# Three planner prices, the choice of the planner's pass, and elementwise work moved from GpSimd to VectorE

## The chip, the cores and the metric

The program runs on one core of one Trainium2 chip. The metric is the device time of one execution in microseconds; the kernel before was timed three times and its median is used.

## The reference, cut to what matters

A linear attention with a decaying state over 768 steps (4 batches, 8 heads, head size 40) feeds two feed-forward layers of 320 by 2048, with different gates.

```python
for t in range(S):                                    # S = 768, state is D x D per head
    y[:, :, t] = einsum('bhd,bhde->bhe', rt, state)
    Sa = einsum('bhde,bhe->bhd', state, at)
    state = state * wt[:, :, None, :] - einsum('bhd,bhe->bhde', Sa, bt) + einsum('bhd,bhe->bhde', vt, kt)
x = y.transpose(0, 2, 1, 3).reshape(3072, 320)
h = x @ moe_w_in;  x = (h * cos(h)) @ moe_w_out
h = x @ moe2_w_in; x = (h * clip(h + 3, 0, 6) / 6) @ moe2_w_out
```

The feed-forward weights arrive as 64-bit floats.

## The kernel before

The sequence is cut into 12 chunks of 64 steps; a chunk and a batch together are a unit `n` (48 of them). For each unit the attention loads operands (`pA`), scales and splits them into two fp16 parts (`pB`), transposes them by DMA (`pT`), forms a 64 by 64 system (`pC`), and later solves and applies it (`cV`, `cU`, `cA`, `cG`, `cF`); the state between chunks is carried in `S8` (`cS`, `cF`), and its fp16 copies go out by `cST`. Per chunk, `iA` to `iC` invert triangular blocks on VectorE, column by column, and `iD`/`iE` join the blocks with 64 small fp32 products of 32 by 32 (32 calls each, four partition groups, tile `q`), which give the tile `TT`.

The feed-forward layers run per chunk: `mA` forms `h` in PSUM (16 matmuls of 128 by 128 by 256), applies the gate on ScalarE and VectorE and splits the result into `ghl`; `mB` multiplies it with `wout` into `acc`. Layer 0 and layer 1 alternate on TensorE with the attention of later chunks.

The weights come in 44 pieces (22 per layer). `ld_w` loads a piece as pairs of 32-bit words, `prep_w` builds fp32 values from them: ScalarE takes the absolute value of the high word, VectorE shifts (`tensor_scalar`) and puts the sign in, and then the top three bits of the low word have to come in. Since `E_LO` is 1 for both layers, `cnt` always reaches 1 and this last step goes by ScalarE (a scaled copy of the low word to an integer) and an integer add on GpSimd. After that a cast and a subtraction make the two fp16 parts.

No engine's order is written by hand. All calls go to a recorder, `Plan`: `rec` gives each a price in ns, `order` works out an order, and `emit` issues it. Lines that matter:

```python
ALTS = {"ANY": ("DVE", "POOL"), "CPY": ("DVE", "ACT")}
```

A call on `nc.either` that isn't a copy has the engine ANY, and one that is a copy has CPY: the planner chooses the engine as it goes. `order` alternates 50 times (`PASSES`) between `forward`, a list schedule in modelled time by priority, and `backward`, which gives the next priorities; the start times of the last `forward` are the order, and the engine of each ANY and CPY call is the one of that pass. In `forward`, `pick` gives GpSimd an ANY call when VectorE isn't running an operation marked `port` (no operand in PSUM), and only if `o["alt"] - spare <= POOL_GAIN * o["c"]`; while GpSimd runs, VectorE gets calls without that mark alone. The order has no effect on the chip but through the sequence on each engine and on the SP queue, which issues nearly all DMAs; semaphores do the rest.

The price of a DMA on SP's queue is 475 or 650 by the partitions of its tile, and 1175 or 1244 for a transposing one. A fp32 matmul costs `max(2 * (5 + 0.835 * m), 4 * n / 2.4)`, which is 63.4 for the 32 by 32 product; the shape change adds 192 to a block of them. Every operation is issued through line 459 (or 455, where a copy falls to ScalarE), so the profile's groups are told apart by tile names. Tile `wstat` is a second staging place beside `wout`; `Tt` also holds the fp16 state parts, `S8a` also the small tiles `xs` and `ul`.

Of the kernel before, what the change touches and what calls it, by code (L numbers as in the profile page):

```python
# [12 lines left out]
U32 = mybir.dt.uint32  # L13
AF = mybir.ActivationFunctionType
ALU = mybir.AluOpType
# [23 lines left out]
W_HUGE = 122880.0  # L39
W_SCALE = 2.0 ** -111  # L40
W_TOP = 2.0 ** -96
E_LO = 1.0, 1.0
T_R, T_0, T_D1, T_D2, T_W0, T_W0E, T_W1, T_W1E = 78, 70, -8, -6, -59, -30, -5, 11
T_P, D_P, T_I, D_I, T_C, D_C, T_M2, T_WM, LAG = 48.0, 2.0, 36.0, 7.0, 26.05, 2.1, 8, 150, 2
E_WC, E_WL, E_DM, E_NT, E_GL, E_KB, E_AR, E_XS, E_MA = 1, 0, 0, 0, 0.5, 0, 0, 0, 0
# [32 lines left out]
        return t  # L78


ALTS = {"ANY": ("DVE", "POOL"), "CPY": ("DVE", "ACT")}
T_SHAPE = 96.0
FULL = (128, 128)
POOL_GAIN = -0.03
OFFSET = 110
LAT = {"PE": 190, "DVE": 125, "ACT": 140, "POOL": 70}

# [1 line left out]
class Plan:  # L89
# [68 lines left out]
    def rec(self, attr, eng, name, a, kw):  # L158
        i = len(self.ops)
        outs, ins = [], []  # L160
        if a and isinstance(a[0], bass.AP):
            outs.append(a[0])
            ins += [x for x in a[1:] if isinstance(x, bass.AP)]
        for k, x in kw.items():
            if isinstance(x, bass.AP):
                (outs if k in ("out", "accum_out") else ins).append(x)
        n = max(_free(x) for x in outs[:1] + (ins if name in ("tensor_reduce", "activation") else []))
        dma = None
        if name.startswith("dma"):
            sb = outs[0] if outs[0].tensor.__class__.__name__ == "Tile" and outs[0].tensor._space != DRAM else ins[0]  # L170
            c = 475.0 if sb.shape[0] in (32, 128) or ins[0].ap[0][0] == 0 else 650.0
            by = 1
            for k in outs[0].shape:
                by *= k
            by *= mybir.dt.size(outs[0].dtype)
            if name == "dma_start":
                run = _run(outs[0], ins[0])
                run = min(run, 20480)
                dma = by / run * (9 + run * 0.045) / 16
            else:  # L180
                r, w = ins[0].shape[0], by // 2 // ins[0].shape[0]
                dma = w / 128 * 204 * (1 if r >= 64 else r / 128)
                c = 1244.0 if r == 128 and w >= 1024 else 1175.0
        elif eng == "PE":
            m = _free(ins[0])
            c = max(n / 2.4 + 2.5, 25.0 if m == 128 else 32.0)
            if ins[0].dtype == F32:
                c = max(2 * (5 + 0.835 * m), 4 * n / 2.4)
            shape = tuple(32 if x <= 32 else 64 if x <= 64 else 128 for x in (ins[0].shape[0], _free(ins[0])))
        elif eng in ("DVE", "ANY"):  # L190
            c = 70 + n * 1.042
            es = max(mybir.dt.size(x.dtype) for x in outs + ins)
            if name == "tensor_copy":
                c = 70 + n * (0.26 if es == 2 else 0.52)
            elif name == "tensor_tensor" and n > 512 and any(len(x.ap) > 2 and abs(x.ap[-1][0]) > 4 for x in ins):
                c = 70 + n * 1.906
            elif name == "tensor_scalar":
                c = 70 + n * 0.52
            elif name == "reciprocal":
                c = 70 + n * 6.3  # L200
            elif name == "tensor_tensor_scan":
                c = 70 + n * 2.08
            if any(_free(x) == 1 for x in ins):
                c += 60
        elif eng == "ACT":
            c = 95 + n * 0.833
            if "accum_out" in kw:
                c += 93
            elif "bias" in kw:
                c += 50  # L210
            elif ins[0].tensor._space == PSUM:
                c -= 42

        turn = name == "tensor_copy" and n > 512 and abs(outs[0].ap[-1][0]) > 4
        if turn:
            c = 70 + n * 1.906
        rate = 2.56 if any(abs(x.ap[-1][0]) > 4 for x in ins) else 2.1 if all(mybir.dt.size(x.dtype) == 4 for x in outs + ins) else 1.88
        cp = 36 + n * 0.83 if name == "memset" else 150 + n * (rate if name == "tensor_tensor" else 3.4)
        if eng == "POOL":
            c = cp  # L220
        elif eng == "ANY" and name == "tensor_copy":
            eng, cp = "CPY", 70 + n * 1.906 if turn else 95 + n * 0.833
        merge = eng == "PE" and self.ops and self.ops[-1]["eng"] == "PE" and self.ops[-1]["grp"] == (self.group, outs[0].tensor.name)
        if merge:
            i -= 1
            o = self.ops[i]
            o["c"] += c + (T_SHAPE if shape != o["shape"] else 0)
            o["shape"] = shape
        else:
            o = dict(eng=eng, c=c, alt=cp if eng in ALTS else None, dma=dma, deps=set(), prio=self.prio, calls=[],  # L230
                     grp=(self.group, outs[0].tensor.name), i=i, port=False, shape=FULL, off=0)
            self.ops.append(o)
            if eng == "PE" and shape != FULL:
                o["c"] += 2 * T_SHAPE
                o["shape"] = shape

            o["off"] = OFFSET if any(_part(x) for x in outs[:1] + ins) else 0
            o["port"] = name not in ("memset", "tensor_reduce", "reciprocal") and all(getattr(x.tensor, "_space", None) != PSUM for x in ins)
        o["calls"].append((attr, name, a, kw))
        for x in ins:  # L240
            self.touch(x, False, i, o["deps"])
        for x in outs:
            self.touch(x, True, i, o["deps"])

    def order(self):

        ops = self.ops
        n = len(ops)
        for o in ops:
            for k in ("c", "alt", "dma"):  # L250
                o[k] = None if o[k] is None else int(o[k] + 0.5)

        known = [0] * n
        pred = []
        users = [[] for _ in ops]
        for o in ops:
            i, a, keep = o["i"], 0, []
            for d in sorted(o["deps"], reverse=True):
                if not a >> d & 1:
                    keep.append(d)  # L260
                    users[d].append(i)
                    a |= known[d] | 1 << d
            known[i] = a
            pred.append(keep)

        tail = [0] * n
        nxt = 0
        for o in reversed(ops):
            i = o["i"]
            m = max([tail[u] for u in users[i]], default=0)  # L270
            moe = o["eng"] == "PE" and o["grp"][0][0] in ("mA", "mB")
            if moe:
                m = max(m, nxt - LAT["PE"])
            tail[i] = m + (o["c"] + LAT.get(o["eng"], 0) if o["dma"] is None else 2200 + o["dma"])
            if moe:
                tail[i] -= o["c"] * SHARE // 100
                nxt = tail[i]
        pr = [-t for t in tail]
        for k in range(PASSES):
            start = self.forward(pr, pred, users)  # L280
            if k < PASSES - 1:
                pr = self.backward(start, pred, users)
        return sorted(range(n), key=lambda i: (start[i], i))

    def backward(self, start, pred, users):
# [61 lines left out]
    def forward(self, pr, pred, users):  # L347

        ops = self.ops
        n = len(ops)  # L350
# [14 lines left out]
        def pick(e, t):  # L365
# [10 lines left out]
            if e == 3:  # L376
                if port[1] > t:
                    return None
                spare = max(0, free[1] - t) + sum(ops[i]["c"] for _, i in q[1] if i not in gone and not ops[i]["port"])
                for _, i in sorted(q[3]):  # L380
                    if i in gone:
                        continue
                    o = ops[i]
                    if o["eng"] == "POOL" or o["alt"] - spare <= POOL_GAIN * o["c"]:
                        return i
                return None
            return q[e][0][1]

        def arrive(u):
# [113 lines left out]
def kernel(  # L503
# [87 lines left out]
    def dp(name, frac):  # L591
        return nc.either

    cnt = {}
    ldq = nc.sync
    tq = nc.sync

# [166 lines left out]
    def prep_w(m, kind, i):  # L764
# [4 lines left out]
        else:  # L769
# [5 lines left out]
            nc.vector.tensor_scalar(out=x, in0=x, scalar1=3, scalar2=None, op0=ALU.logical_shift_left)  # L775
            nc.vector.scalar_tensor_tensor(out=x, in0=hi, scalar=-(1 << 31), in1=x,
                                           op0=ALU.bitwise_and, op1=ALU.bitwise_or)
            cnt[m] = cnt.get(m, 0.0) + E_LO[m]
            if cnt[m] < 0.999:
                nc.vector.scalar_tensor_tensor(out=x.bitcast(U32), in0=lo.bitcast(U32), scalar=29, in1=x.bitcast(U32),  # L780
                                               op0=ALU.logical_shift_right, op1=ALU.bitwise_or)
            else:
                cnt[m] -= 1.0
                nc.scalar.activation(out=lo, in_=lo.bitcast(U32), func=AF.Copy, scale=2.0 ** -29)
                nc.gpsimd.tensor_tensor(out=x, in0=x, in1=lo, op=ALU.add)
        if kind == "i":
            q, k = divmod(i, 3)
            sl = slice(q * 512, q * 512 + 512)
# [725 lines left out]
```

## Time and profile before

| | us |
|---|---|
| median of three runs | 1210.59 (1209.37 to 1214.22) |
| the profiled execution | 1216.33 |
| its span, first to last instruction | 1214.4 |

Busy time of the engines in that span: PE (TensorE) 873.8 us, DVE (VectorE) 1020.0, ACT (ScalarE) 808.1, POOL (GpSimd) 187.0; the mean granted clock of TensorE is 0.945 of 2.4 GHz. A busy time counts an instruction from its start to its end, also where it stood still in between. SPq in a row is SP's queue: the time that SP took to issue a DMA, which the table of busy times leaves out.

### The profile page before, as it was taken

To read this page: it belongs to the slowest core of one execution; us is meant where nothing else is said; L and a number is where in the kernel's file an instruction comes from. 1 tells how busy PE (TensorE), PEld (TensorE's weight loads), DVE (VectorE), ACT (ScalarE), POOL (GpSimd) and SP (SyncE) were. 2 spreads that over 40 slices of the span, in tenths; PEclk is the share of its full clock that TensorE was granted. 3 is DMA by queue.
4 is the path that set the end of the run, shared out by engine and by line. 5 is a ranking of instruction groups with operands and counts; after the bars stand their busy time and mean duration, and the time that the engine had idled before them with its cause. 6 is when DMAs were issued, how large, how long until landed. Compare 5 with 4: busy or idle time off the path is not lost.

```text
span 1214.4 us, 29691 instructions
## 1 busy us (share of the span) xinstructions
PE 873.8 (72%) x11378; PEld 697.5 (57%) x11378; DVE 1020.0 (84%) x2328; ACT 808.1 (67%) x1695; POOL 187.0 (15%) x221
## 2 busy tenths in 40 slices
PE   0000113357967899799897898999979979999994
PEld 0000112355755677587675677776758758778873
DVE  7699999899999899599895899989969969885652
ACT  5563689888887679487595776867857737464341
POOL 3320111232222101020030020200200114200000
PEclk9999999977987999899999899999989989999998
DMA  6998778997878749777578687776775743512010
GB/s 213 243 195 172 167 218 179 207 202 171 176 152 151 146 85 142 159 130 135 121 128 148 121 144 152 132 148 109 140 162 101 110 99 69 104 37 49 1 25 15
DMA packets 477818, 162.65 MB, mean 134 GB/s; under 512 B 447941, under 2 KB 460273, under 8 KB 477282
## 3 DMA queue, kind: packets, MB, share of 16 engines
q1 hardware_dynamic: 477378, 160.00, 65.9%
q8 instruction: 91, 1.49, 0.5%
q14 instruction: 61, 0.50, 0.2%
q10 hardware_dynamic: 288, 0.67, 0.1%
HBM read 80.09 MB, written 25.61 MB: 87 GB/s over the span
## 4 chain that ended last, share of the span: by engine, by line
DVE 28%; PE 20%; DMA 9%; SPq 6%; issue 5%; ACT 4%; POOL 1%; DVEq 0%; ACTq 0%; POOLq 0%
PE h L459 10%; PE acc L459 7%; SPq L459 6%; DVE Tt L459 4%; DVE s L459 4%; DVE tmp L459 3%; DVE ghl L459 3%; DVE S8a L459 3%; PE t L459 2%; DMA x1T<-S8a 2%; DVE GF L459 1%; DVE FS L459 1%; DVE gm L459 1%; DMA Lt<-Ls 1%; DVE xy L459 1%
## 5 line engine op out<-in xcount | busy, mean ns | idle before, releaser
L459 PE MATMUL acc<-wout,ghl 128*128 128x320 f16 x2304 | 363.3, 306 | 15.5 <-DVE ghl L459 8.3
L459 PEld LDWEIGHTS <-win 128*128 128x128 f16 x3328 | 317.7, 103 | 86.9 <-issue 39.4
L459 PEld LDWEIGHTS <-ghl 128*128 128x128 f16 x2304 | 218.6, 100 | 98.5 <-DVE ghl L459 11.2
L459 PE MATMUL h<-x1T,win 128*128 128x256 f16 (+1 forms) x1664 | 206.1, 287 | 32.6 <-DVE s L459 25.1
L459 ACT ACTIVATE s<-h,cvec 128x512 f32<-128x512 f32 x192 | 130.5, 682 | 136.6 <-PE h L459 66.7
L459 PE MATMUL h<-x2T,win 128*128 128x256 f16 (+1 forms) x1664 | 184.7, 266 | 3.7 <-DVE s L459 3.7
L459 DVE TENSOR_TENSOR ghl<-s,ghl 128x512 f16<-128x512 f32 x177 | 122.0, 690 | 3.2 <-ACT ghl L455 1.4
L459 DVE TENSOR_TENSOR tmp<-Tt,Lt 128x126 f32<-128x126 f32 (+22 forms) x372 | 100.5, 270 | 13.0 <-DMA Lt<-Ls 8.1
L459 DVE TENSOR_TENSOR Tt<-Tt,tmp 128x126 f32<-128x126 f32 (+22 forms) x372 | 103.4, 278 | 4.4
L459 DVE SCALAR_TENSOR_TENSOR s<-h,s 128x512 f32<-128x512 f32 x96 | 65.5, 686 | 42.3 <-ACT s L459 40.5
L459 PE MATMUL p<-ART,KBT 120*128 120x64 f16 x384 | 22.3, 208 | 104.5 <-DMA ART<-ARs 73.3
L455 ACT ACTIVATE ghl<-s 128x512 f16<-128x512 f32 x126 | 78.3, 624 | 27.6 <-DVE s L459 21.4
L459 DVE SCALAR_TENSOR_TENSOR s<-s,h 128x512 f32<-128x512 f32 x96 | 64.8, 678 | 25.0 <-ACT s L459 25.0
L459 PEld LDWEIGHTS <-KBT 120*128 120x128 f16 x384 | 19.6, 107 | 108.6 <-DMA KBT<-KBs 88.7
L459 PE MATMUL t<-E,GF 128*128 128x40 f16 x1152 | 45.7, 183 | 37.7 <-DVE GF L459 37.3
L459 PE MATMUL t<-FS,NT 128*128 128x40 f16 x768 | 37.5, 183 | 37.8 <-DVE FS L459 19.5
L459 PEld LDWEIGHTS <-GF 128*128 128x128 f16 x1152 | 38.0, 98 | 45.7 <-DVE GF L459 25.5
L459 PEld LDWEIGHTS <-TT 64*128 64x128 f16 (+1 forms) x768 | 28.2, 97 | 61.1 <-issue 28.7
L459 POOL TENSOR_TENSOR wout<-wout 128x512 int32<-128x512 int32 (+1 forms) x28 | 45.6, 1637 | 97.7 <-ACT wout L459 72.1
L459 PEld LDWEIGHTS <-NT 128*128 128x128 f16 x768 | 32.6, 98 | 35.4 <-issue 27.2
L459 PEld LDWEIGHTS <-ART 120*64 120x64 f16 (+1 forms) x704 | 43.6, 106 | 7.9 <-issue 4.1
L459 PE MATMUL q<-Lt 32*32 32x32 f32 x1536 | 23.9, 204 | 31.3 <-DMA Lt<-Tm 13.9
(159 smaller groups left out, 1675.1 us busy)
## 6 DMA issues: line engine op xcount, KB each, us to landing
raw<-in_arbk_dram SPq DMA_DIRECT2D x46, 320.0 KB
v<-in_vv_dram SPq DMA_DIRECT2D x96, 80.0 KB
pip<-Dec SPq DMA_DIRECT2D x46, 160.0 KB
wout<-in_moe_w_in_dram SPq DMA_DIRECT2D x12, 512.0 KB
Ls<-LN SPq DMA_DIRECT2D x48, 128.0 KB
Lt<-Ls SPq DMA_DIRECT2D x48, 128.0 KB
TT<-Thl SPq DMA_DIRECT2D x12, 512.0 KB
wstat<-in_moe_w_out_dram SPq DMA_DIRECT2D x10, 512.0 KB
```

The source lines that it names most:

```text
L455: self.nc.scalar.activation(func=AF.Copy, **kw)
L459: getattr(getattr(self.nc, attr), name)(*a, **kw)
```

## The change

Six edits. (1) ANY may go to VectorE alone, and the rule with `POOL_GAIN` goes. (2) In `prep_w` the low word's bits come in with one VectorE `scalar_tensor_tensor` (shift right by 29, or) in place of the ScalarE copy and the GpSimd add; `E_LO` and `cnt` go. (3) A plain DMA costs 520, 640, 740 or 960 ns of SP's queue by the number of contiguous runs and the partitions. (4) A transposing DMA costs 1310 or 1390. (5) A fp32 matmul with 32 columns of weights costs 30. (6) `order` keeps the start times and the engines of the pass with the smallest modelled last start.

```diff
-ALTS = {"ANY": ("DVE", "POOL"), "CPY": ("DVE", "ACT")}
+ALTS = {"ANY": ("DVE",), "CPY": ("DVE", "ACT")}
-POOL_GAIN = -0.03
...
-            c = 475.0 if sb.shape[0] in (32, 128) or ins[0].ap[0][0] == 0 else 650.0
...
+                k = by // run
+                c = 520.0 if k <= 64 else 640.0 if k <= 128 else 960.0 if sb.shape[0] == 40 else 740.0
                 run = min(run, 20480)
...
-                c = 1244.0 if r == 128 and w >= 1024 else 1175.0
+                c = 1390.0 if r == 128 and w >= 1024 else 1310.0
...
-                c = max(2 * (5 + 0.835 * m), 4 * n / 2.4)
+                c = 30.0 if m == 32 else max(2 * (5 + 0.835 * m), 4 * n / 2.4)
...
+        best = None
         for k in range(PASSES):
             start = self.forward(pr, pred, users)
+            if best is None or max(start) < best[0]:
+                best = max(start), start, [o["on"] for o in ops]
             if k < PASSES - 1:
                 pr = self.backward(start, pred, users)
+        _, start, on = best
+        for o, e in zip(ops, on):
+            o["on"] = e
...
-                spare = max(0, free[1] - t) + sum(ops[i]["c"] for _, i in q[1] if i not in gone and not ops[i]["port"])
-                for _, i in sorted(q[3]):
-                    if i in gone:
-                        continue
-                    o = ops[i]
-                    if o["eng"] == "POOL" or o["alt"] - spare <= POOL_GAIN * o["c"]:
-                        return i
-                return None
             return q[e][0][1]
...
-            cnt[m] = cnt.get(m, 0.0) + E_LO[m]
-            if cnt[m] < 0.999:
-                nc.vector.scalar_tensor_tensor(out=x.bitcast(U32), in0=lo.bitcast(U32), scalar=29, in1=x.bitcast(U32),
-                                               op0=ALU.logical_shift_right, op1=ALU.bitwise_or)
-            else:
-                cnt[m] -= 1.0
-                nc.scalar.activation(out=lo, in_=lo.bitcast(U32), func=AF.Copy, scale=2.0 ** -29)
-                nc.gpsimd.tensor_tensor(out=x, in0=x, in1=lo, op=ALU.add)
+            nc.vector.scalar_tensor_tensor(out=x.bitcast(U32), in0=lo.bitcast(U32), scalar=29, in1=x.bitcast(U32),
+                                           op0=ALU.logical_shift_right, op1=ALU.bitwise_or)
```

## Rows read from the trace of the kernel before

**Rows 1.** The page: busy shares in 40 slices of the span, in tenths.

```profile
PE   0000113357967899799897898999979979999994
...
DVE  7699999899999899599895899989969969885652
...
POOL 3320111232222101020030020200200114200000
PEclk9999999977987999899999899999989989999998
```

**Rows 2.** Busy time of each engine in three stretches of the span.

```profile
0.00:400.00 400.00, 148.76 (x2344) 122.74 (x2345) 360.81 (x744) 288.30 (x585) 95.99 (x102) 0.92 0.83 187
400.00:1100.00 700.00, 627.02 (x8161) 497.35 (x8159) 603.59 (x1472) 483.77 (x1037) 90.96 (x119) 0.96 0.67 122
1100.00:1214.40 114.40, 97.99 (x880) 77.43 (x878) 55.57 (x113) 36.08 (x74) 0.00 (x0) 0.95 0.10 20
```

**Rows 3.** The page: the chain that ended last, share of the span.

```profile
DVE 28%; PE 20%; DMA 9%; SPq 6%; issue 5%; ACT 4%; POOL 1%; DVEq 0%; ACTq 0%; POOLq 0%
```

**Rows 4.** Groups of POOL by form: count, busy us, mean ns, idle before.

```profile
L459 POOL TENSOR_TENSOR wout<-wout 128x512 int32<-128x512 int32 x22 | 35.3, 1606 | 88.7 <-ACT wout L459 70.2 <-DVE NT L459 7.1 <-issue 5.1
L459 POOL TENSOR_TENSOR wstat<-wstat 128x512 int32<-128x512 int32 x14 | 21.4, 1529 | 107.4 <-ACT wstat L459 34.4 <-DVE tmp L459 29.7 <-DVE S8a L459 20.0
L459 POOL TENSOR_TENSOR S8a<-S8a,pd 40x320 f32<-40x320 f32 x19 | 20.0, 1059 | 47.1 <-DMA pd<-Ds 46.4
L459 POOL TENSOR_TENSOR ghl<-s,ghl 128x512 f16<-128x512 f32 x15 | 17.7, 1183 | 48.0 <-ACT ghl L455 35.7 <-DVE ghl L459 5.9 <-DVE tmp L459 4.4
```

**Rows 5.** Timeline of DVE and POOL at three places.

```profile
28.43 1.51 DVE L459 TENSOR_SCALAR wout<-wout 64x512 int32<-64x512 int32 x1
...
255.03 3.19 POOL L459 TENSOR_TENSOR wout<-wout 128x512 int32<-128x512 int32 x2 [6.24 <-ACT wout L459]
255.30 1.78 DVE L459 SCALAR_TENSOR_TENSOR wout<-wout 128x512 int32<-128x512 int32 x1
257.01 2.73 DVE L459 TENSOR_SCALAR wstat<-wstat 64x512 int32<-64x512 int32 x1
...
1039.89 0.44 DVE L459 TENSOR_TENSOR tmp<-Tt,Lt 128x108 f32<-128x108 f32 x1
```

**Rows 6.** DVE's instructions by tile: ns minimum/median/maximum, first and last start.

```profile
L459 DVE SCALAR_TENSOR_TENSOR wout<-wout x28: 661/684/1779, 27.2 to 346.3; 128x512 int32<-128x512 int32 x22, 64x512 int32<-64x512 int32 x6
L459 DVE TENSOR_TENSOR ghl<-s,ghl x177: 670/684/1785, 245.6 to 1194.6; 128x512 f16<-128x512 f32 x177
L459 DVE TENSOR_TENSOR S8a<-S8a,pd x21: 484/490/1467, 226.3 to 967.5; 40x320 f32<-40x320 f32 x21
```

**Rows 7.** ScalarE's preparation of `wout` by tile, and copies by either engine.

```profile
L459 ACT ACTIVATE wout<-wout x56: 639/660/692, 12.7 to 346.1; 128x512 f32<-128x512 f32 x22, 128x512 int32<-128x512 uint32 x22, 64x512 f32<-64x512 f32 x6, 64x512 int32<-64x512 uint32 x6
...
L459 DVE CAST ghl<-s x66: 404/426/465, 402.3 to 1190.4; 128x512 f16<-128x512 f32 x66
...
L455 ACT ACTIVATE ghl<-s 128x512 f16<-128x512 f32 x126 | 78.3, 624 | 27.6 <-DVE s L459 21.4 <-PE acc L459 2.9 <-DVE Tt L459 2.2
```

**Rows 8.** The fp32 products: busy time over the span, then two places of PE's timeline.

```profile
0.00:1214.40 1214.40, 23.95 (x1536) 0.94 0.67 134
...
333.88 0.75 PE L459 MATMUL q<-Lt 32*32 32x32 f32 x64
...
136.00 1.08 PE L459 MATMUL q<-Lt 32*32 32x32 f32 x64 [4.11 <-ACT Lt L459]
```

**Rows 9.** SP's issues by tile: ns minimum/median/maximum.

```profile
L459 SPq DMA_TRANSPOSE KBT<-KBs x48: 1231/1300/3869, 48.4 to 961.1; - x48
L459 SPq DMA_DIRECT2D Srep<-Tt x66: 770/857/1406, 205.4 to 1048.1; - x66
L459 SPq DMA_DIRECT2D v<-in_vv_dram x96: 466/582/2096, 7.4 to 1082.1; - x96
L459 SPq DMA_DIRECT2D Lt<-Tm x48: 325/426/1407, 127.1 to 1058.8; - x48
```

**Rows 10.** The chain in order of time, two pieces near the end: start, us, what.

```profile
1143.04 1.63 PE acc L459 x12
1144.67 1.75 PE h L459 x16
```

More of the change, by code (lines that the diff above doesn't have):

```diff
@@ L41 @@
 W_TOP = 2.0 ** -96
-E_LO = 1.0, 1.0
 T_R, T_0, T_D1, T_D2, T_W0, T_W0E, T_W1, T_W1E = 78, 70, -8, -6, -59, -30, -5, 11
@@ L592, in dp @@
         return nc.either
-    cnt = {}
     ldq = nc.sync
```

## Prediction

> **What bounds the kernel now.** I began with the busy shares over the span [rows 1]. Three stretches show. In the first third VectorE is the full engine and TensorE the empty one; in the middle TensorE is at 9 in most slices and VectorE at 8 to 9; at the end TensorE alone is full. With the numbers [rows 2]: up to 400 us DVE is busy 360.8 of 400 (90%) and PE 148.8; from 400 to 1100 PE is busy 627.0 of 700 (90%) and DVE 603.6 (86%); after 1100 PE has 98.0 of 114.4 and DVE half. So the start belongs to VectorE, the middle is shared, and the end is a chain on TensorE that this change hardly touches. The chain that ended last [rows 3] says the same: DVE 28% of the span, PE 20%, then waits on transfers 9% and SP's queue 6%, which is 0.06 x 1214 = about 75 us in which the chain stood at SP issuing; POOL has 1%, 12 us.
>
> Then I asked what GpSimd's work costs VectorE. Here the reader is to see something that the busy shares hide. At 255.03 POOL starts two integer adds that take 3.19 us together; the DVE operation at 255.30 takes 1.78 us where its median is 0.684, and the next takes 2.73 [rows 5, 6]. Over the whole trace 76 DVE instructions last over 0.1 us longer than the median of their kind while a POOL tensor operation runs beside them; the first is at 28.43 and the last at 1039.89 [rows 5]. One instruction alone is that late without POOL. Summed, the 76 are 53.3 us late, 34.2 of it before 400 us and 19.1 after. POOL is late in the same way: its integer adds take 1.27 us at the least and 1.53 to 1.61 on average [rows 4].
>
> **The change part by part.** *The integer adds.* 44 of them leave POOL (22 and 14 of the two main groups [rows 4], and 8 of 64 partitions), all before 400 us. In their place come 44 DVE `scalar_tensor_tensor` on the same words. The nearest row is the sign step on the same tile, 0.684 us: 44 x 0.684 = 30.1 us more DVE. 44 ScalarE copies go at 0.66 us [rows 7]: 29 us less ACT, all before 400 us. Their cover would have been ACT's 28% idle time there, so their removal is worth something only through what ACT takes over.
>
> *The ANY calls.* The other 91 POOL tensor operations go to DVE: 15 of the `ghl` kind at 0.684 = 10.3; 49 on 40 partitions (19 for `S8a<-S8a,pd`, and 15 each of two more kinds) at 0.490 = 24.0; and 27 of kinds between these two prices, 14.5 [rows 4, 6]. That is 48.8 us, 6.1 for the 12 that start before 400 us and 42.7 for the 79 after. On POOL these took 0.8 to 1.2 us each, so where one of them stands in a chain (the state `S8a`, `ghl` ahead of `mB`) its result comes about 0.4 us sooner once DVE starts it. POOL keeps its memsets, 187.0 less 168 = 19 us, which only write; those of `iA` were queued behind elementwise work and are free now.
>
> *Sum on VectorE.* Before 400 us: 30.1 + 6.1 - 34.2 = +2. After: 42.7 - 19.1 = +23.6. So VectorE gets nothing back as a whole, and the question is where the surplus lies.
>
> *First stretch.* With ACT 29 us lighter, the planner may give it casts that DVE had. A cast of 128 by 512 is 0.624 us on ACT and 0.426 on DVE [rows 7], so 29 us hold at most 46 casts, which take 20 us off DVE. Bounds: +2 (no cast moves) to 2 - 20 = -18. DVE is not busy for 39 us of that stretch, so not all of it reaches the end. I take -8.
>
> *Middle stretch.* +23.6 us on an engine with 700 - 603.6 = 96 us idle. The work that hides it is PE's, 90% busy; if that cover is gone it costs all 24. Bounds 0 to +24. Since the idle time is four times what is added, I take a quarter, +6.
>
> The Trainium skill speaks against this part in one sentence (Perfetto Trace Analysis, section Optimizing Scalar/DVE Operations): where VectorE is saturated, moving work to ScalarE or even GpSimd may make sense, though it warns that the two share a read port and that it may not help. By its first half the sum for VectorE would be +79 us; the rows above, with 53.3 of it given back, side with the warning.
>
> *Prices of SP's queue.* Nothing about a transfer changes but the order in which things are issued. For 20 kinds of transfer, 862 of the 939 issues, the old prices add up to 656 us, the new ones to 747, and SP really took 752 (summed over the issues in the trace; four of the kinds, with their counts and medians, stand in [rows 9]). So the planner believed SP 13% faster than it is, and from 400 to 900 us SP was busy issuing for four fifths of the time. Kind by kind the new prices aren't all better: `KBT` 1244 became 1390 with a median of 1300, `Srep` 650 became 960 with 857, `Lt<-Tm` 475 became 740 with 426, `v` 650 became 520 with 582 [rows 9]. What improves is that a transfer is no longer planned ahead of what SP can issue, so engines aren't told to take first an item whose data comes late. Bounds: a gain of at most the 75 us that the chain spends at SP; a loss of 48 x 0.31 = 15 us if the overpriced `Lt<-Tm` is held back each time. I take a fifth of the 75, -15. Where this stall goes, the next thing late is the transfer itself (DMA, 9% of the chain), which no price shortens.
>
> *The price of fp32 products.* A block of 32 calls was planned at 32 x 63.4 + 192 = 2.22 us and is now at 32 x 30 + 192 = 1.15. The chip took 23.95 us for all 24 blocks, 1.0 each, 0.75 to 1.08 in the timeline [rows 8]. The plan gets 24 x 1.07 = 26 us of PE back that the chip never spent. Bounds 0 to -26; the products stand between waits for transfers and for ScalarE, so I take -2.
>
> *The best pass.* No row shows a pass. What two passes differ in is which item takes a slot; the coarse slot is one `h` block and one `acc` block, 1.75 + 1.63 = 3.4 us of the chain [rows 10]. I bound it by none to four slots, 0 to -14, and take one, -4; the modelled end is not the chip's end.
>
> *Sum.* -8 + 6 - 15 - 2 - 4 = -23 us. Against the profiled execution, 1216.3, that gives 1193; that execution lies 5.7 above the median of the three runs, so on the median's scale it is **1188 us**.
>
> **The rivals.** *No change.* PE is 90% busy in the middle, and the chain there changes hands in pieces of a microsecond or two; a truer order then only shifts which wait ends last. The start gives its 8 us, the middle takes 6 and the plan is worth nothing: 1204 to 1217. For it: the sum for VectorE is about even. Against it: SP's 75 us of the chain are real waits.
>
> *Slower: VectorE becomes the bound of the middle.* The 23.6 us come on the path in full, the start gives nothing (+2), and the prices give 4: 1211 + 22 = 1233. It decides from the point where DVE's share from 400 to 1100 us passes that of PE, about 90%: 603.6 + 23.6 = 627.2, exactly PE's 627.0. So this isn't far, and what speaks against it is that copies can still go to ScalarE, at 484 of 700 us there.
>
> *Slower: the late time doesn't come back.* If the 76 late instructions were late for another reason that stays, VectorE gets all 79 us. In the first stretch 360.8 + 36.2 = 397 of 400, so those 36 us come on the path, and a quarter of the 42.7 after: 1211 + 36 + 11 = 1258. That is what the first half of the skill's sentence (the same page) would give. Against it stands the one late instruction without POOL.
>
> *A larger gain.* If the order was the true fault, half of SP's 75 us goes (-37), all of the first stretch's bound (-18), -8 for the products and -10 for the pass, with +6: 1211 - 67 = 1144, or any part of the way.
>
> **How the numbers follow.** My forecast, from a smaller to a fuller gain than the sum, 1168 to 1204: 0.54. Larger gain, 1140 to 1168: 0.12. No change: 0.17. VectorE the bound, 1217 to 1240: 0.12. Late time stays, above 1240: 0.05. A measurement of this kernel tells about 0.5%, 6 us, from no change. So faster 0.54 + 0.12 = 0.66, same 0.17, slower 0.17. The range leaves out the last rival, a good half of the one before and a quarter of the larger gain: 1155 to 1224; the forecast's own range is 1168 to 1204.
>
> **What would show it.** Right: POOL near 19 us; no DVE instruction far above its kind's median; 44 new `scalar_tensor_tensor` near 0.68 us; DVE near 1045 less the casts that ACT took; less SPq in the chain. The gain should lie in two places, the time at which `mA` of chunk 0 starts and the stretch from 400 to 1100. Wrong: DVE above PE in the middle with PE waiting for `ghl`, `GF` or `S8a`; SPq's share unchanged; or late DVE instructions with POOL idle.

## The result: 1175 us, 3.1% faster

The changed kernel takes 1175.19 us as the median of four executions, against 1211.74 for four of the kernel before; the ratio is 0.9688, with a 95% interval from 0.9654 to 0.9723. One of the four executions took 3814.94 us; it is left out of the ratio, and its cause was not looked into. The profiled execution took 1171.65 us, with a span of 1169.6.

The page after, busy shares in 40 slices, and the chain's shares:

```profile
PE   0010133833777988999879998999899899999993
...
DVE  7689989889999989899899998899989979898552
...
POOL 2000000000000000000000000000000000000000
...
DVE 31%; PE 20%; DMA 9%; ACT 5%; issue 5%; SPq 2%; DVEq 0%; ACTq 0%
```

Busy time after, in the stretches of [rows 2] (the last one ends with the span):

```profile
0.00:400.00 400.00, 161.19 (x2478) 132.06 (x2479) 357.97 (x803) 283.06 (x572) 12.17 (x46) 0.91 0.83 187
400.00:1100.00 700.00, 644.26 (x8453) 517.48 (x8451) 633.76 (x1562) 502.01 (x1073) 8.09 (x40) 0.97 0.68 124
1100.00:1169.60 69.60, 51.70 (x451) 39.88 (x449) 27.85 (x62) 21.38 (x45) 0.00 (x0) 0.90 0.08 17
```

The count behind PE's busy time is the one to read: it says how far the work has come. Up to 400 us TensorE has issued 2478 matmuls against 2344 before, and from 400 to 1100 us 8453 against 8161 [rows 2]. Both stretches are denser: 134 matmuls more by 400 us and 292 more after, which at the 11.7 per us of the middle before are an estimated 11 and 25 us. In the middle VectorE rose from 86% to 91%. The 11378 matmuls of both kernels kept TensorE busy for 857.1 us against 873.8; how much of that belongs to its granted clock (0.97 in the middle against 0.96) no run tells apart.

The prediction looked for the gain at the start of `mA` of chunk 0 and in the stretch from 400 to 1100 us. That start, the first time in each line below (the kernel before, then the changed one), comes 42 us earlier, though the count above makes it 11 us of work by 400 us; the larger part is won in the second place.

```profile
L459 PE MATMUL h<-x1T,win x1664: 216/273/421, 231.8 to 1136.0; 128*128 128x256 f16 x156, 128*128 128x128 f16 x29
```

```profile
L456 PE MATMUL h<-x1T,win x1664: 217/272/421, 189.8 to 1089.7; 128*128 128x256 f16 x156, 128*128 128x128 f16 x29
```

VectorE after, by tile (ns minimum/median/maximum):

```profile
L456 DVE SCALAR_TENSOR_TENSOR wout<-wout x56: 667/678/693, 26.2 to 338.7; 128x512 int32<-128x512 int32 x22, 128x512 uint32<-128x512 uint32 x22, 64x512 int32<-64x512 int32 x6, 64x512 uint32<-64x512 uint32 x6
...
L456 DVE TENSOR_TENSOR win<-wout,win x18: 674/684/687, 31.5 to 309.0; 128x512 f16<-128x512 f32 x12, 64x512 f16<-64x512 f32 x6
```

The largest sign or low-word step now takes 0.693 us, where one took 1.779 [rows 6]. Over the whole trace no VectorE instruction lasts more than 0.1 us above the median of its kind; before there were 77, 53.4 us together.

What meets the eye is the change on VectorE. The experiments ask how much of the gain belongs to it.

### The profile page after: what moved, and what is told of

Its sections match the earlier page's. It is cut to its first block, busy times and chain, and to the rows that moved or that the text cites. A ratio compares the mean times of both kernels' runs of the same rounds, so it can differ in the third digit from the quotient of the medians.

```text
span 1169.6 us, 29485 instructions
## 1 busy us (share of the span) xinstructions
PE 857.1 (73%) x11378; PEld 689.4 (59%) x11378; DVE 1019.6 (87%) x2425; ACT 806.5 (69%) x1689; POOL 20.3 (2%) x86
## 4 chain that ended last, share of the span: by engine, by line
DVE 31%; PE 20%; DMA 9%; ACT 5%; issue 5%; SPq 2%; DVEq 0%; ACTq 0%
PE h L456 9%; PE acc L456 8%; DVE Tt L456 4%; DVE s L456 4%; DVE ghl L456 4%; DVE S8a L456 4%; DVE tmp L456 3%; SPq L456 2%; PE t L456 2%; DVE GF L456 2%; DMA raw<-in_arbk_dram 2%; DVE FS L456 2%; DVE gm L456 2%; DMA v<-in_vv_dram 2%; DMA TT<-Thl 1%
## 5 line engine op out<-in xcount | busy, mean ns | idle before, releaser
L456 PEld LDWEIGHTS <-win 128*128 128x128 f16 x3328 | 309.5, 100 | 68.6 <-issue 27.5
L456 PE MATMUL h<-x1T,win 128*128 128x256 f16 (+1 forms) x1664 | 186.7, 270 | 18.0 <-DVE s L456 9.1
L456 PE MATMUL h<-x2T,win 128*128 128x256 f16 (+1 forms) x1664 | 190.0, 271 | 7.3 <-DVE s L456 6.6
L456 DVE TENSOR_TENSOR ghl<-s,ghl 128x512 f16<-128x512 f32 x192 | 130.9, 684 | 4.7 <-ACT ghl L452 2.6
L452 ACT ACTIVATE ghl<-s 128x512 f16<-128x512 f32 x139 | 86.6, 624 | 35.7 <-DVE s L456 30.1
L456 DVE TENSOR_TENSOR tmp<-Tt,Lt 128x126 f32<-128x126 f32 (+22 forms) x372 | 91.9, 247 | 9.0 <-DMA Lt<-Ls 5.7
L456 DVE TENSOR_TENSOR Tt<-Tt,tmp 128x126 f32<-128x126 f32 (+22 forms) x372 | 91.6, 246 | 3.5
L456 DVE TENSOR_TENSOR raw<-raw,pip 128x640 f32<-128x640 f32 x46 | 37.6, 817 | 7.6 <-DMA raw<-in_arbk_dram 4.9
L456 ACT ACTIVATE FS<-v 128x640 f16<-128x640 f32 x48 | 35.0, 728 | 10.1 <-DMA v<-in_vv_dram 9.0
```

The lines of the kernel that those rows point to most:

```text
L452: self.nc.scalar.activation(func=AF.Copy, **kw)
L456: getattr(getattr(self.nc, attr), name)(*a, **kw)
```

## The experiments

Twelve kernels ran, four to a chip, and each time the kernel before ran beside them (medians 1213.95, 1215.51 and 1216.06 us); the ratios are to those. In brackets stands the 95% interval. "Modelled last start" is a figure of the planner's own plan and no time of the chip.

**1. Edits 1 and 2 alone.**

```diff
-ALTS = {"ANY": ("DVE", "POOL"), "CPY": ("DVE", "ACT")}
+ALTS = {"ANY": ("DVE",), "CPY": ("DVE", "ACT")}
...
+            nc.vector.scalar_tensor_tensor(out=x.bitcast(U32), in0=lo.bitcast(U32), scalar=29, in1=x.bitcast(U32),
+                                           op0=ALU.logical_shift_right, op1=ALU.bitwise_or)
```

> The kernel before with edits 1 and 2 alone: no elementwise work on GpSimd, the old prices, the last pass. Theory G (the gain comes from GpSimd's work leaving: the 53 us of late VectorE instructions go, and the plan holds on the chip): most of the 36 us, 1175 to 1190 us. Theory P (the gain comes from the prices of SP's queue and of the fp32 products): within 8 us of before, 1203 to 1220, since VectorE gets 25 us more work and nothing else is better. Theory S (any new order moves the time by this much, whatever the reason): no forecast, anywhere from 1170 to 1240.

1187.96 us, 0.9804 [0.9777, 0.9831]. Two thirds of the change's gain, as theory G wants it. Taken by itself it would have closed the case.

**2. Edits 3, 4 and 5 alone.**

```diff
+                k = by // run
+                c = 520.0 if k <= 64 else 640.0 if k <= 128 else 960.0 if sb.shape[0] == 40 else 740.0
...
-                c = 1244.0 if r == 128 and w >= 1024 else 1175.0
+                c = 1390.0 if r == 128 and w >= 1024 else 1310.0
...
+                c = 30.0 if m == 32 else max(2 * (5 + 0.835 * m), 4 * n / 2.4)
```

> The kernel before with edits 3, 4 and 5 alone: the new prices of SP's queue and of the fp32 products, GpSimd still with its elementwise work, the last pass. Theory G: the late VectorE instructions stay near 50 us, so 1203 or more. Theory P: 1175 to 1190, with SP's queue down from 6% of the chain. If both count, 1188 to 1200.

1163.54 us, 0.9601 [0.9571, 0.9630]: faster than the whole change, with GpSimd as busy as before. Its `ghl` subtraction on VectorE and its busy times (as in [rows 2], with a middle of 600 us):

```profile
L460 DVE TENSOR_TENSOR ghl<-s,ghl x175: 673/685/1770, 220.1 to 1139.9; 128x512 f16<-128x512 f32 x175
```

```profile
0.00:400.00 400.00, 155.60 (x2457) 128.06 (x2458) 371.06 (x752) 310.56 (x630) 101.13 (x107) 0.90 0.84 191
400.00:1000.00 600.00, 553.71 (x7411) 444.65 (x7409) 547.34 (x1341) 448.69 (x970) 75.93 (x98) 0.99 0.74 135
```

The late instructions are all there (a maximum of 1.770 us for an operation of 0.685; 87 instructions are over 0.1 us late, 63.7 us in all, more than before, and 83 of them overlap a tensor operation of GpSimd), and the kernel is 48 us faster on the scale of the ratio. Theory G can't stand as the whole.

**3. Edit 6 alone.**

```diff
+            if best is None or max(start) < best[0]:
+                best = max(start), start, [o["on"] for o in ops]
```

> The kernel before with edit 6 alone: the best of 50 passes by the planner's own reckoning, whose modelled last start is 1094.9 us against 1104.6 of the last pass. If the model's difference carried over whole: 1201. Theories G and P: 1200 to 1214, little. Theory S: it may fall anywhere from 1190 to 1230, since it is another order with equal prices.

1191.88 us, 0.9831 [0.9802, 0.9860]: 22 us for a modelled 9.7. That is a gain on the kernel before, and it is also a measure of how much the choice of a pass can move at equal prices. In the changed kernel edit 6 does nothing: with its prices the last of the 50 passes happens to be the one with the smallest last start (1104.6), so that the kernel without this edit has the same order.

**4. The plan before, GpSimd's operations issued on VectorE at their places.**

```diff
+            if o["on"] == "POOL" and name == "tensor_tensor":
+                if kw["out"].dtype == I32:
+                    kw = dict(kw, op=ALU.bitwise_or)
+                self.nc.vector.tensor_tensor(*a, **kw)
```

> The plan of the kernel before, unchanged, but each GpSimd tensor operation is issued on VectorE at the place that its planned start gives it (the integer adds as a bitwise or of the same words; ScalarE's copies of the low word stay). It takes the late instructions away and leaves the order on TensorE, ScalarE and SP's queue as it was. If the late instructions themselves are the cost: VectorE +25 us net and still faster, 1180 to 1200. If GpSimd's leaving pays only through a new plan: 1208 to 1235, since VectorE has 25 us more in an order that was made for it without them.

1217.45 us, 1.0026 [1.0004, 1.0047]. Engine totals, the `ghl` subtraction and the busy times:

```profile
PE 881.8 (72%) x11378; PEld 700.3 (58%) x11378; DVE 1039.5 (85%) x2463; ACT 812.1 (67%) x1695; POOL 20.1 (2%) x86
```

```profile
L463 DVE TENSOR_TENSOR ghl<-s,ghl x177: 672/685/694, 239.0 to 1196.7; 128x512 f16<-128x512 f32 x177
```

```profile
0.00:400.00 400.00, 157.86 (x2400) 129.12 (x2401) 365.64 (x826) 298.69 (x608) 11.45 (x46) 0.93 0.87 191
400.00:1000.00 600.00, 533.72 (x6928) 420.65 (x6927) 524.64 (x1316) 418.53 (x883) 8.66 (x40) 0.95 0.70 129
```

The late time is gone (maximum 0.694 us) and VectorE has 1039.5 us against 1020.0: +19.5, where I had worked out +25. The time is that of before, at most half a per cent worse. What one takes and the other gives cancel in the time, as they nearly do in the sum for VectorE. What either of them costs by itself this run can't tell: both changed together. So taking the late time away isn't enough for run 1's gain of 26 us; it came with the new plan. By its length that plan promises nothing (its modelled last start is 1115.5 us, 11 more than before), so the chip came nearer to the plan. Two reasons are not told apart: a plan that knows of no late instructions is kept better without them, and the 44 copies that run 1 takes off ScalarE stay in run 4.

**5 and 6. The two kinds of price, each alone.** Run 5 has edit 5, run 6 edits 3 and 4, in the form shown for run 2.

> The kernel before with edit 5 alone, the price of the 32 by 32 fp32 products (30 in place of 63.4); SP's prices stay. Modelled last start 1075.7 us against 1104.6 before. If the product's price is what helped in the run with prices alone (its modelled gain carried over whole): 1180 to 1190. If SP's prices were what helped, as my prediction had it (15 us for SP, 2 for the products): 1205 to 1215.

> The kernel before with edits 3 and 4 alone, the prices of SP's queue; the product's price stays. Modelled last start 1090.8 us. If SP's prices are what helped: 1175 to 1195, with the chain's SPq share below 6%. If the product's price was: 1200 to 1214.

The product's price: 1180.27 us, 0.9712 [0.9675, 0.9748]. SP's prices: 1178.23 us, 0.9704 [0.9675, 0.9732]. Each gives about 35 us on the kernel before, nearly as much as the whole change; together (run 2) they give 48.

A part of how a price that changes no duration saves time can be read where the products' results are waited for. The line below is from the view of tile `q`, list of who waited for it: us, times. `PE t` are the products of `cU` and `cA` behind the blocks; the operation that they wait for is the copy of `q` into `TT` by ScalarE or its second part by VectorE. The kernels are the one before, run 6, run 5, run 2 and the changed one, in this order.

```profile
PE t L459: 25.0, 24
```

```profile
PE t L460: 29.7, 27
```

```profile
PE t L459: 9.4, 16
```

```profile
PE t L460: 5.0, 7
```

```profile
PE t L456: 5.4, 10
```

In the first two, with the old price, TensorE stands 25.0 and 29.7 us behind these blocks, 1.0 to 1.1 us each time on average; in the other three, with the new one, 5 to 9. In the other kernels too the two groups keep apart: 11.6 to 21.6 us with the old price (runs 1, 3, 4, 7 and 12), 5.5 to 7.6 with the new (runs 8 to 11). The old plan held 2.22 us for a block that takes 1.0 [rows 8], and what followed was put in an order that fits a later end. On the chip the block ends 1.1 us sooner, so the plan has too little other work to cover the copies behind it, and TensorE waits. That last step is my reading of the order and was not tested by itself. The wait doesn't account for the whole gain either: from the kernel before to run 5 it falls by 15.6 us, and the time by 35. Nor is it one wait for each block, though both count 24: in the kernel before single ones last from 0.15 to 4.8 us, up to three behind one pair of blocks.

**7 and 8. How far do two orders of one modelled length lie apart?**

```diff
-PASSES = 50
+PASSES = 17
```

> The kernel before with 17 passes in place of 50 and nothing else: another order of the same work at the same prices, whose modelled last start (1104.4 us) is within 0.2 us of that before (1104.6). It measures how far two orders of equal modelled length lie apart on the chip. If the model's order of merit holds: 1205 to 1220. If orders scatter by as much as single edits moved the time: anywhere from 1185 to 1240, and an edit's 20 us is then not a proof of its mechanism.

> The changed kernel with 35 passes in place of 50 and nothing else. It keeps its pass 34, with a modelled last start of 1105.2 us, where the changed kernel keeps its last pass with 1104.6. The scatter on the other side: 1170 to 1181 if equal modelled length means equal time; 1160 to 1195 if orders scatter.

Run 7: 1219.56 us, 1.0046 [1.0020, 1.0072] of before. Run 8 (the changed kernel with 35 passes): 1170.74 us, 0.9648 [0.9613, 0.9683], where the changed kernel has 0.9688. So another order of equal modelled length is worth 0.4 to 0.5%, 5 us, in these two pairs. Two pairs are few, and run 3 is a warning: same prices, another pass, and 22 us, 12 more than its model says. So up to that much can come from the pass alone. The kernels without edit 6 keep the last pass, whatever it is worth. Measured against run 3 in place of the kernel before, run 5 is 1.2% faster (0.9712 / 0.9831), run 6 1.3% (0.9704 / 0.9831), and run 1 0.3%, which is nothing. So each price alone is worth between 1.2 and 3%, and that edits 1 and 2 help the plan of before isn't shown. What stands clear of this are the two prices together: with the best pass on both sides (run 10 against run 3) they give 3.7% (0.9467 / 0.9831).

**9. The changed kernel with edit 1 undone; 10. with edits 1 and 2 undone.**

```diff
-ALTS = {"ANY": ("DVE",), "CPY": ("DVE", "ACT")}
+ALTS = {"ANY": ("DVE", "POOL"), "CPY": ("DVE", "ACT")}
+POOL_GAIN = -0.03
...
+                    if o["eng"] == "POOL" or o["alt"] - spare <= POOL_GAIN * o["c"]:
+                        return i
```

> The changed kernel with edit 1 undone: the ANY calls may go to GpSimd again; the integer adds stay on VectorE, all prices and the best pass stay. Modelled last start 1061.4 us against 1104.6 of the changed kernel. If the ANY calls' leaving is a cost of the change (with the prices alone and GpSimd busy the time was 1163.5, below the changed kernel's 1175): 1150 to 1166. If it is a gain: 1180 or more.

> The changed kernel with edits 1 and 2 undone: GpSimd has all its elementwise work, new prices, best pass (modelled last start 1064.8 us; the last pass, run before, has 1072.5 and took 1163.5). If the best pass carries its modelled 7.7 us over: 1155; if it is worth nothing: 1158 to 1169, which is the scatter of two orders of one modelled length seen so far (5 us).

Run 9: 1144.40 us, 0.9401 [0.9361, 0.9441]. Run 10: 1152.94 us, 0.9467 [0.9429, 0.9506]. Both beat the changed kernel. Edit 1 costs 0.9688 / 0.9401 = 1.031, 3%, where all else is as in the change; edits 1 and 2 together cost 0.9688 / 0.9467 = 1.023. All three keep the best pass. The prices, for their part, add less once edits 1 and 2 are in: the changed kernel is 1.2% faster than run 1 (0.9688 / 0.9804). The gains of the parts don't add up. The busy times of run 9, and then of the changed kernel in the same middle stretch:

```profile
0.00:400.00 400.00, 165.00 (x2661) 137.19 (x2662) 369.90 (x815) 292.63 (x598) 55.57 (x82) 0.92 0.89 197
400.00:1000.00 600.00, 561.50 (x7500) 450.78 (x7497) 548.97 (x1324) 458.81 (x984) 85.43 (x110) 0.99 0.76 134
```

```profile
400.00:1000.00 600.00, 546.07 (x7292) 437.76 (x7290) 549.55 (x1400) 451.22 (x964) 8.09 (x40) 0.97 0.75 136
```

VectorE is equally busy in both, 549 of 600 us, 92%; with it run 9 gets 7500 matmuls done against 7292, and GpSimd carries 85 us of work beside it. Its late instructions are 38.1 us in all, and it is the faster of the two all the same.

**11. The plan of run 2, GpSimd's operations issued on VectorE at their places** (the edit of run 4 on top of run 2).

> The plan of the run with prices alone, unchanged, with each GpSimd tensor operation issued on VectorE at the place of its planned start (integer adds as a bitwise or). In that run 63 us of late time came with GpSimd's work, and 77 us of work would go to VectorE, net +14. If late instructions cost nothing on balance, as in the same trial on the plan of before: 1160 to 1172. If they are a loss that a tight plan feels: below 1158. If VectorE, 92% busy in the middle there, is the bound: above 1175.

1164.38 us, 0.9574 [0.9545, 0.9603]; run 2 had 0.9601, measured on another chip. Its middle:

```profile
400.00:1000.00 600.00, 551.63 (x7357) 439.99 (x7355) 555.13 (x1388) 446.97 (x962) 7.53 (x35) 0.99 0.74 133
```

So the finding of run 4 holds in a tighter plan as well: moving the work changes nothing that can be told from noise. And a kernel whose GpSimd is empty can run at 1164 us, with VectorE at 93%, if its plan was made with GpSimd in it. This speaks for the plan that is found without GpSimd as what edit 1 costs (modelled last start 1104.6 against 1072.5 for run 2 and 1061.4 for run 9), and against VectorE's load as such. It isn't shown for run 9 itself: whether its plan would also bear its GpSimd work on VectorE wasn't tried.

**12. SP's prices too high.**

```diff
+            c *= 1.25
```

(on run 6, for every DMA)

> The kernel before with the new prices of SP's queue times 1.25 (sum some 930 us for transfers that took 752); the product's price as before. If the prices help because they are near what SP takes, overpricing gives a good part of the gain of the run with SP's prices (1178) back: 1190 to 1225. If a dearer SP queue helps as such, by bringing loads forward: 1165 to 1182.

1204.50 us, 0.9905 [0.9859, 0.9951]. Three points on one scale: planned sums for the same transfers of 656, 747 and some 930 us give ratios of 1, 0.9704 and 0.9905, and the chip took 752. Near what SP takes is better than too high by 2% and better than too low by 1.3% (against run 3) to 3%, with one order for each point. It isn't dearness that helps.

**Plan and chip side by side.** The orders by modelled last start, in us:

| order | modelled | measured | difference |
|---|---|---|---|
| before; other pass (7); best pass (3) | 1104.6; 1104.4; 1094.9 | 1214; 1220; 1192 | 109; 115; 97 |
| edits 1 and 2 (1) | 1115.5 | 1188 | 72 |
| product's price (5) | 1075.7 | 1180 | 105 |
| SP's prices (6); the same times 1.25 (12) | 1090.8; 1153.2 | 1178; 1205 | 87; 51 |
| both (2); and best pass (10) | 1072.5; 1064.8 | 1164; 1153 | 91; 88 |
| both, low word on DVE, best pass (9) | 1061.4 | 1144 | 83 |
| changed kernel; other pass (8) | 1104.6; 1105.2 | 1175; 1171 | 71; 66 |

The two prices work in two ways. The product's price makes the plan shorter by 29 us and leaves the difference (105). SP's prices bring the chip nearer to the plan by some 20 us, and times 1.25 nearer still, but then the plan is 49 us longer than before. That run 6's plan is also 14 us shorter than before can't come from dearer transfers; it is the luck of the search. Edit 1 brings the chip nearer by 12 us (run 9 against the changed kernel), but the plan itself grows by 43 us, and that is the larger number.

## Why the prediction was right, and which of its steps were wrong

The time lies in the range, the sign is right, and so is the main idea: the sum put 17 of its 23 us on truer prices. That the sum (-23) came as near as it did to the measured -36.5 is in part luck, since errors of opposite sign cancel in it: the prices together gave 48 us (run 2), and on top of them edits 1 and 2, put at -2 together, cost 2.3% (run 10 against the changed kernel).

- *The price of fp32 products* is the worst term: -2 in the sum, -35 alone on the kernel before (-14 against its best pass). I bounded the gain with the plan's surplus (26 us), a bound that -35 breaks, and then valued it at next to nothing because the products stand between other waits. The rows on tile `q` show that TensorE waited 15.6 us less behind them; where the rest of the gain lies stays open.
- *SP's prices*: -15 in the sum, -36 alone on the kernel before (-15 against its best pass, run 3). The mechanism, a plan in which SP is 13% too fast, fits run 12, where prices too high lose as well. The measure that I took, a fifth of the chain's 75 us at SP, was poor: run 5, which has the old prices of SP, gains as much. SPq's share in the chain fell to 2% in the changed kernel, as I had said it would, but that proves little.
- *The late VectorE instructions*: count, cause and return were right (77 to none, 53 us; POOL 20.3 us, forecast 19; the low-word step at 0.68 us). The balance too: +19.5 us on VectorE with the plan held. On the time the swap of late time for work is even (runs 4 and 11: +0.3%, and nothing). The first stretch's -8 can't be checked by itself: all edits together gave it an estimated 11 us, and run 4 leaves ScalarE's copies in. ScalarE took 38 copies over from VectorE over the whole kernel (247 to 209), so its busy time stayed at 806.5 instead of falling by 29. I had reckoned with 46 at most.
- *The middle stretch*: +6 for 24 us more on VectorE. My slower rival was to decide where VectorE passes TensorE from 400 to 1100 us. It did not: VectorE has 633.8 us there and TensorE 644.3 (only up to 1000 us is VectorE ahead, 549.6 to 546.1). Edit 1 does cost 3% against run 9, but hardly in the way of this rival: run 9 has VectorE as busy, and run 11, at 93%, is faster than the changed kernel (0.9574 against 0.9688). What the sum has no term for is that the planner finds a longer plan without GpSimd.
- *The best pass*: -4 in the sum, nothing in this kernel, 22 us on the kernel before.
- *The sentence on GpSimd* (the Trainium skill, Perfetto Trace Analysis, section Optimizing Scalar/DVE Operations), that a saturated VectorE may be relieved by GpSimd though it might not help, was nearer the mark than I made it: with 38 us of late instructions in it, run 9 is the fastest kernel of all. The warning of the Trainium skill in that section, that it might not help, holds where the plan is kept (runs 4 and 11: no difference).

## What to carry to other kernels

A planner's price that is too high can cost more than the operation itself: what stands around it is ordered for a later end than the real one. So compare each price with the trace, those of small operations and of a DMA queue's issue time included, and try both sides of the right value. When an edit changes a resource and the plan at once, also run the old plan with the new resource: here the visible story (late instructions beside GpSimd's) turned out even with what it takes to remove them. And before a gain is put down to an edit, run another order at the same prices: here that alone moved the time by up to 22 us.

## What the runs showed of the hardware

While GpSimd ran a tensor operation with inputs in SBUF, VectorE operations beside it took up to 3.003 us in place of 0.685 (`win<-wout,win`, before), and GpSimd's integer add, 1.27 us at the least, took up to 2.99 (128 partitions). Without GpSimd's work the same group on VectorE has a maximum of 0.687 us. Before:

```profile
L459 DVE TENSOR_TENSOR win<-wout,win x18: 678/685/3003, 34.7 to 314.7; 128x512 f16<-128x512 f32 x12, 64x512 f16<-64x512 f32 x6
```

The size was unexpected, and so was that the kernel took the same time within half a per cent whether it had these 53 us or, in the same plan, some 20 us more of busy VectorE in their place.
